# The attention product's way from PSUM into two time mixes, with a new order list and other cuts of the token axis

## The chip, the cores and the metric

The kernel runs on one core of a Trainium2 chip. The metric is the device time of one execution in microseconds (us). Engines go by the names of the profile: TensorE (PE, with its weight loads as PEld), VectorE (DVE), ScalarE (ACT), GpSimd (POOL) and SyncE (SP), which only issues transfers.

## The reference

Three stages follow each other. B = 2 batches, H = 12 heads, S = 448 tokens, D = 64.

```python
# 1: causal attention, float32
scores = q @ k.T / 8, masked above the diagonal; attn = exp(scores - rowmax)
attn = attn / (sum(attn) + 1e-9); x = (attn @ v) as (B, S, 768)

# 2: a feed-forward stage with a time mix
x_prev = x shifted by one token, a zero row first
xk = mu_k * x + (1 - mu_k) * x_prev
xr = mu_r * x + (1 - mu_r) * x_prev
v = relu(xk @ w_k) ** 2 @ w_v          # w_k 768 x 1024, w_v 1024 x 768
x = sigmoid(xr @ w_r) * v              # w_r 768 x 768

# 3: a feed-forward stage with a convolution over tokens
h = relu(x @ w_in); gate = sigmoid(conv3(h)); out = (h * gate) @ w_out
```

The weight matrices and the convolution weights arrive as 64-bit floats; the kernel turns them into 32-bit by integer steps.

## The kernel before

**Attention.** The 24 heads are worked as 12 jobs of two heads each: jobs 0 to 5 are batch 0, jobs 6 to 11 batch 1, and job i holds the 128 columns number i mod 6 of x. A job loads raw q and k (`Lk`) and v (`Lv`), transposes q and k on TensorE (`kqT`, line 313), copies them out of PSUM (`kC`), makes the scores in two groups (`sc.1`, `sc.2`, line 334), and for each of seven row blocks takes the row maximum with the mask (`red`, VectorE, line 347), the exponential with its sum (`exp`, ScalarE, line 356) and the scaling by the reciprocal sum (`norm`, line 72, 74 or 76 by engine). The scaled blocks are transposed (`T.a`, `T.b`, line 376), copied out (`C`), and multiplied with v into one PSUM bank po (`V.a`, `V.b`, line 404): x transposed, channels on the partitions, one zero column ahead of the 448 tokens, so that the shifted x is a slice of the same bank.

**The time mix.** From po, `mP.1` scales the shifted x by 1 - mu_r into a work tile m, `mD.1` adds mu_r times x (VectorE, line 429): that is xr. `mP.0` and `mD.0` do the same with mu_k into the kept tile `mixed`: that is xk. All four read po, so its bank is free when the fourth is done. `mH` and `mL` split xr into a high part (rounded to the format of the products) and a low rest; `k0` to `k11` with `H` and `L` do that for xk, once the attention's memory has been given over to the later stage (`act2`).

**Products.** Each product of the later stages is three matmuls (high by high, high by low, low by high; `mm3`, line 66). `pr e.b.c` is the part of xr @ w_r for output slice e, batch b and channel slice c; `E0` to `E3` are xk @ w_k for output slices 0 and 1 and both batches (PSUM tiles pk). In these the 896 tokens are cut as 448 and 448 (`TOK`). All later products cut them as 512 and 384 (`HALF`). A weight slice goes through the steps `L` (load), `a` (absolute value, ScalarE, line 137), `b`, `c`, `d`, `e` (integer steps), `h` and `l` (split).

**Order.** Around the change the order is written out by hand: in the string `ORDER` each word is one step, its engine after a slash (a, v or p), and TensorE, ScalarE, VectorE and GpSimd each run their steps in that order. SyncE's transfers are kept in the order of the text. After `E3` a planner orders the next stage (products pk and pv), and a second hand list orders the last one.

## Time and profile before

| | us |
|---|---|
| median of 3 runs | 354.12 (353.56 to 354.26) |
| the profiled execution, its own time | 353.53 |
| its span, first to last instruction | 351.8 |
| PE busy in the span | 345.7 |
| DVE busy | 307.2 |
| ACT busy | 235.2 |
| POOL busy | 94.9 |

The profile is of one execution. Busy times are sums over the span. Matmuls overlap each other, and their ends are modelled, so what a matmul costs is the distance from its start to the next start, and a busy PE can still hold short waits. On ScalarE and VectorE the end of one instruction overlaps the start of the next as well, and again the distance between starts is its cost.

### The profile page before, as it was taken

To read this page: it belongs to the slowest core of one execution; us is meant where nothing else is said; L and a number is where in the kernel's file an instruction comes from. 1 tells how busy PE (TensorE), PEld (TensorE's weight loads), DVE (VectorE), ACT (ScalarE), POOL (GpSimd) and SP (SyncE) were. 2 spreads that over 40 slices of the span, in tenths; PEclk is the share of its full clock that TensorE was granted. 3 is DMA by queue.
4 is the path that set the end of the run, shared out by engine and by line. 5 is a ranking of instruction groups with operands and counts; after the bars stand their busy time and mean duration, and the time that the engine had idled before them with its cause. 6 is when DMAs were issued, how large, how long until landed. Compare 5 with 4: busy or idle time off the path is not lost.

```text
span 351.8 us, 7217 instructions
## 1 busy us (share of the span) xinstructions
PE 345.7 (98%) x2682; PEld 309.5 (88%) x2682; DVE 307.2 (87%) x630; ACT 235.2 (67%) x515; POOL 94.9 (27%) x155
## 2 busy tenths in 40 slices
PE   8999999999999999999999999999999999999995
PEld 7678788888999998998888999998988999999995
DVE  3999999999989877989999997998998999898731
ACT  3999999999543276767886464345757878766501
POOL 8486986677535000000000000000000000368100
PEclk9999999999999999999999999999999999999999
DMA  7975855342033155446455434444231200379623
GB/s 180 250 161 124 203 137 163 76 133 76 11 93 113 56 179 181 131 140 238 155 174 182 148 100 170 150 133 167 89 108 73 89 2 0 67 135 214 128 89 135
DMA packets 60320, 45.33 MB, mean 129 GB/s; under 512 B 31608, under 2 KB 59036, under 8 KB 60284
## 3 DMA queue, kind: packets, MB, share of 16 engines
q1 hardware_dynamic: 56140, 39.90, 37.5%
q0 software_dynamic: 3216, 4.74, 7.3%
q8 instruction: 21, 0.34, 0.4%
q10 hardware_dynamic: 928, 0.23, 0.3%
q14 instruction: 15, 0.12, 0.1%
HBM read 38.17 MB, written 2.75 MB: 116 GB/s over the span
## 4 chain that ended last, share of the span: by engine, by line
PE 94%; ACT 2%; DVE 2%; POOL 1%; issue 0%; POOLq 0%
PE pk L66 17%; PE pv L66 16%; PE pr L66 13%; PE A L66 7%; PE po L404 6%; PE s L334 4%; PE B L66 4%; PE c L66 2%; PE D L66 2%; PE Yb L376 2%; PE Xa L376 2%; PE W L574 1%; PE q L313 1%; PE ph5l L66 1%; PE ph4l L66 1%; PE ph6l L66 1%
## 5 line engine op out<-in xcount | busy, mean ns | idle before, releaser
L903 POOL DMA_DIRECT2D s<-g x12 | 12.9, 1196 | 194.9 <-ACT st L87 188.6
L356 ACT ACTIVATE p<-e,st 128x448 f32<-128x448 f32 (+6 forms) x84 | 42.4, 514 | 1.9 <-DVE st L347 1.6
L72 POOL TENSOR_SCALAR p<-p,st 128x64 f32<-128x64 f32 (+6 forms) x70 | 34.7, 513 | 15.5 <-DVE st L347 6.1
L347 DVE CUSTOM_DVE_ANT_0 e<-s,mask 128x192 f32<-128x192 f32 (+6 forms) x84 | 31.5, 412 | 0.4 <-ACT p L356 0.4
L404 PE MATMUL po<-pt,v 128*64 128x128 f32 (+4 forms) x384 | 24.0, 277 | 0.0
L404 PEld LDWEIGHTS po<-pt,v 128*64 128x64 f32 x384 | 20.0, 137 | 3.3 <-issue 0.3
L334 PE MATMUL s<-kT,qT 64*64 64x384 f32 (+6 forms) x336 | 22.1, 386 | 0.7 <-DVE kT L79 0.5
L823 DVE SCALAR_TENSOR_TENSOR cv<-hT,cw,cv 128x448 f32<-128x448 f32 x32 | 21.5, 679 | 1.4 <-ACT cv L820 1.4
L334 PEld LDWEIGHTS s<-kT,qT 64*64 64x64 f32 x336 | 14.9, 132 | 6.8 <-ACT qT L79 0.9
L356 ACT ACTIVATION_READ_ACCUMULATOR p<-e,st 128x1 f32 x84 | 17.0, 202 | 0.0
L87 ACT ACTIVATE x<-xv 128x512 fp32r<-128x512 f32 (+1 forms) x12 | 6.8, 573 | 9.2 <-DVE xv L722 9.2
L91 POOL TENSOR_TENSOR xr<-m,xr 128x448 fp32r<-128x448 f32 x10 | 12.0, 1200 | 2.1 <-ACT xr L87 1.7
L1015 ACT ACTIVATE o<-A 128x384 f32<-128x384 f32 x3 | 1.5, 491 | 14.7 <-PE A L66 14.6
L827 ACT ACTIVATE cv<-cv 128x448 f32<-128x448 f32 x16 | 9.1, 571 | 3.2 <-DVE cv L823 3.2
L820 ACT ACTIVATE cv<-hT,cw 128x448 f32<-128x448 f32 x16 | 10.7, 668 | 0.5 <-DVE g L91 0.3
L829 DVE TENSOR_TENSOR cv<-cv,hT 128x448 f32<-128x448 f32 x16 | 9.9, 618 | 1.2 <-ACT cv L827 1.2
L903 POOL DMA_DIRECT2D wo6raw<-g x8 | 9.1, 1187 | 3.9 <-ACT wo6raw L928 3.9
L91 DVE TENSOR_TENSOR k<-a,k 128x512 fp32r<-128x512 f32 (+2 forms) x16 | 9.9, 617 | 0.0
L66 PE MATMUL pv<-k,wv0hl 128*128 128x512 f32 (+1 forms) x48 | 9.9, 364 | 0.0
L66 PE MATMUL pv<-k,wv4hl 128*128 128x512 f32 (+1 forms) x48 | 9.8, 363 | 0.0
L66 PE MATMUL pv<-k,wv2hl 128*128 128x512 f32 (+1 forms) x48 | 9.8, 363 | 0.0
L66 PE MATMUL pv<-k,wv3hl 128*128 128x512 f32 (+1 forms) x48 | 9.8, 363 | 0.0
(518 smaller groups left out, 1111.7 us busy)
## 6 DMA issues: line engine op xcount, KB each, us to landing
rqk<-in_q_dram SPq DMA_DIRECT2D x23, 112.0 KB, 3.4
v<-in_v_dram SPq DMA_DIRECT2D x24, 96.0 KB, 2.9
s<-g POOLq DMA_DIRECT2D x12, 192.0 KB, 3.8
rqk<-in_k_dram SPq DMA_DIRECT2D x16, 112.0 KB, 3.1
wo6raw<-g POOLq DMA_DIRECT2D x8, 192.0 KB, 4.9
wv0raw<-in_moe_w_v_dram SPq DMA_DIRECT2D x1, 1024.0 KB, 5.0
wv1raw<-in_moe_w_v_dram SPq DMA_DIRECT2D x1, 1024.0 KB, 4.6
wv2raw<-in_moe_w_v_dram SPq DMA_DIRECT2D x1, 1024.0 KB, 4.8
```

Of the source, the lines that this page charges most:

```text
L66: nc.tensor.matmul(ps_out, x, y, start=first and i == 0, stop=last and i == 2, skip_group_check=more,)
L72: nc.gpsimd.tensor_scalar(out_, in_, s, 1.0, ALU.mult, ALU.mult)
L91: e.tensor_tensor(out_, x, f32(h), ALU.subtract)
L334: nc.tensor.matmul(held[self.name(f"s{f}")][1][h, o:z], qT[r, i * LO:(i + 1) * LO], kT[r, :(i + 1) * LO], start=True, stop=True,)
L347: nc.vector.tensor_tensor_reduce(t[:, :w], used(self.name(f"s{f}"))[:, o:z], mask[:, S - w:], -SCALE, 3e38, ALU.add, ALU.min, self.st[:, 0 ...
L356: nc.scalar.activation(p[:, :w], self.s[i][:, :w], AF.Exp, bias=self.st[:, 0, i:i + 1], scale=-1.0, accum_out=self.st[:, 1, i:i + 1],)
L376: nc.tensor.transpose(o[:, u * LO:(u + 1) * LO], self.p[i][r, k0:k0 + P], ident[r, r])
L404: nc.tensor.matmul(self.T["po"][j * D:(j + 1) * D, 1 + i * LO - z:1 + (i + n) * LO], self.v[:, kc, j], self.T["pt"][:, a - z:a + n * LO], ...
L820: nc.scalar.activation(a, x[:, 0:S], AF.Copy, scale=cw[:, f:f + 1])
L823: nc.vector.scalar_tensor_tensor(a, x[:, j:S + j], cw[:, j * NF + f:j * NF + f + 1], a, ALU.mult, ALU.add)
L829: (nc.gpsimd if eng == "p" else nc.vector).tensor_tensor(a, a, hc, ALU.mult)
L903: nc.gpsimd.dma_start(out=dst, in_=f32(x), accum_op=ALU.add)
```

## The change

The product po is read three times instead of four: `xC` copies x (448 columns) from PSUM into `mixed`; `mP` makes the scaled shifted x for xr, from po (ScalarE, VectorE) or, where its engine is GpSimd, from the copy; `mD` adds as before. The key path's mix is now two steps of the k family on the copy: `P` scales the shifted copy into a work tile (447 columns) and scales column 0 in place, `D` adds mu_k times the copy in place (VectorE, both inputs in SBUF). These stand late in the order.

The cuts `TOK` give way to `PART`, 384 and 512 tokens, in the products pr, in E0 to E3, in the copies `sr` and in what reads pk 0 and 1; the second part holds the last 64 tokens of batch 0. In the new list five of the twelve `mP` run on GpSimd, four of nine weight slices do step `a` and four do step `h` on VectorE; ScalarE does 14 norms instead of 7; six of the twelve xk steps `H` are on VectorE and all twelve `L`; six of the xr steps `L` are on VectorE instead of two. The loads of job 1 stand ahead of those of job 0, and job 1 to 3's k loads are words of their own (`Lp`). The tiles of the later stage are all named at `act2`, in the order in which they were first used before; v's buffers are named ahead of those of raw q and k. The whole order list is new.

```diff
-    def narrow(step, dst, raw, eng="v"):
+    def narrow(step, dst, raw, eng=""):
 
         lo, hi = raw[:, 0::2], raw[:, 1::2]
         d = dst.bitcast(I32)
         if step == "a":
-            in_order(nc.scalar.activation(dst, hi.bitcast(F32), AF.Abs))
+            if eng == "v":
+                nc.vector.tensor_scalar(d, hi, as_int(0x7FFFFFFF), None, ALU.bitwise_and)
+            else:
+                in_order(nc.scalar.activation(dst, hi.bitcast(F32), AF.Abs))
+    vs = Kept(rawp, "v", 4, [P, NB + 1, 2, D], lambda t: [t[:LO, NB]])
...
     TOK = [slice(b * S, (b + 1) * S) for b in range(B)]
+    PART = [slice(0, 3 * P), slice(3 * P, NT)]
+
+    def width(t):
+        return t.stop - t.start
 ...
-    vs = Kept(rawp, "v", 4, [P, NB + 1, 2, D], lambda t: [t[:LO, NB]])
...
         def Lk(self):
             self.raw = first_qk if self.i == 0 else qks.get(self.i, self.name("rqk"))
-            other = nc.scalar if self.i == 0 else nc.gpsimd if self.i < 4 else nc.sync
-            for src, dst, e in ((q, self.raw[:LO], nc.sync), (k, self.raw[LO:], other)):
-                for j in range(2):
-                    if self.i or j == 0 or src is k:
-                        in_order(e.dma_start(out=dst[:, :, j], in_=half(src, self.b, 2 * self.hp + j)))
+            for j in range(2):
+                if self.i or j == 0:
+                    in_order(nc.sync.dma_start(out=self.raw[:LO, :, j], in_=half(q, self.b, 2 * self.hp + j)))
+            if self.i not in (1, 2, 3):
+                self.k_half(nc.sync if self.i else nc.scalar)
+
+        def Lp(self):
+            self.k_half(nc.gpsimd)
+
+        def k_half(self, e):
+            for j in range(2):
+                in_order(e.dma_start(out=self.raw[LO:, :, j], in_=half(k, self.b, 2 * self.hp + j)))
 ...
-                self.T["po"] = bank(self.name("po"), 4)
+                self.T["po"] = bank(self.name("po"), 3)
...
-        def mP(self, eng, kind):
-            kind = int(kind)
-            m = self.m(kind)
-            a = 2 * NC + kind * NC + self.hp
-            scaled(eng, m, used(self.name("po"))[:, :S], mu[:, a:a + 1])
-
-        def m(self, kind):
-            if not kind:
-                return mixed[self.hp][:, self.b]
-            if "m" not in self.T:
-                self.T["m"] = mslots.get(self.i, self.name("m"))
-            return self.T["m"][:, :S]
-
-        def mD(self, _, kind):
-            kind = int(kind)
-            m, a = self.m(kind), kind * NC + self.hp
-            nc.vector.scalar_tensor_tensor(m, used(self.name("po"))[:, 1:S + 1], mu[:, a:a + 1], m, ALU.mult, ALU.add)
+        def xC(self, eng):
+            copy(eng, mixed[self.hp][:, self.b], used(self.name("po"))[:, 1:S + 1])
+
+        def mP(self, eng):
+            self.T["m"] = t = mslots.get(self.i, self.name("m"))
+            x = 3 * NC + self.hp
+            po = used(self.name("po"))
+            if eng == "p":
+                nc.gpsimd.memset(t[:, :1], 0.0)
+                scaled(eng, t[:, 1:S], mixed[self.hp][:, self.b, :S - 1], mu[:, x:x + 1])
+            else:
+                scaled(eng, t[:, :S], po[:, :S], mu[:, x:x + 1])
+
+        def mD(self, _):
+            m, x = self.T["m"][:, :S], NC + self.hp
+            nc.vector.scalar_tensor_tensor(m, used(self.name("po"))[:, 1:S + 1], mu[:, x:x + 1], m, ALU.mult, ALU.add)
 
         def mH(self, eng):
-            mix_h(xr[self.hp], self.m(1), self.b, eng)
+            mix_h(xr[self.hp], self.T["m"][:, :S], self.b, eng)
 
         def mL(self, eng):
-            mix_l(xr[self.hp], self.m(1), self.b, eng)
+            mix_l(xr[self.hp], self.T["m"][:, :S], self.b, eng)
             mslots.put(self.i)
 
     def mix_h(dst, m, b, eng):
-        split_h("p" if eng == "p" else "s", dst[:, 0, TOK[b]], m)
+        split_h(eng, dst[:, 0, TOK[b]], m)
 ...
-                narrow(s, self.c[:, :n], self.raw.bitcast(I32)[:, :2 * n], eng or "v")
+                narrow(s, self.c[:, :n], self.raw.bitcast(I32)[:, :2 * n], eng)
...
-                split_h("s", self.t[:, 0, :n], self.c[:, :n])
+                split_h(eng, self.t[:, 0, :n], self.c[:, :n])
...
     ORDER = """
-        0:Lk W0 sm:L W*2 0:kqT 0:kC.k/a sm:a 1:Lk 0:kC.q/v W*2 0:sc.2 W*1 1:kqT sm:n 0:red.0 0:red.5 0:red.2 0:red.3
-        0:exp.0 0:sc.1 1:kC.k/v 2:Lk pads 0:exp.5 1:kC.q/a 0:exp.2 1:sc.2 0:red.6 0:exp.3 0:red.1 0:red.4 0:exp.1 0:exp.4
...
-        10:V.a w4:b/p w4:c 11:V.b 11:C.aX/a 11:V.a act2 11:mP.1/a 9:mD.1 pr0.1.0 pr0.1.1 w4:d 10:mP.1/v 9:mH/p
-        pr4.0.4 pr5.1.5 pr4.0.5 sr2.1/a pr5.0.4 w7:d sr4.1/v E0 sr5.1/a k10:L/v sr3.1/v k11:L/p sr4.0/a w8:b/v w8:c
...
+        1:Lk 1:Lp 0:Lk sm:L 2:Lk W0 W*2 0:kqT 0:kC.q/a 0:kC.k/v W*1 sm:a sm:n W*2 0:sc.1 0:red.1 1:kqT 0:red.6
+        0:sc.2 0:exp.1 1:kC.q/a 1:kC.k/v 1:sc.2 0:red.4 0:exp.6 0:exp.4 0:red.2 2:Lp 0:red.3 0:red.5 1:red.3
...
+        10:norm.2/p 10:T.b 11:exp.6 11:exp.5 10:norm.0/p 11:exp.1 10:T.a 11:rec 11:norm.5/p w0:h pr1.1.1 pr1.1.2
+        k8:D 10:C.bY/a 11:norm.6/p 11:Lv 11:norm.4/a 10:C.bX/a 11:norm.0/p w5:L 10:C.aY/a w4:c pr2.1.0 9:xC/v
+        9:mP/v 11:norm.1/p 9:mD sr2.0/a pr2.1.1 10:C.aX/a k2:D pr2.1.2 k5:P/a 11:T.a 9:mH/a w0:l/v 11:norm.3/p
+        11:norm.2/a 11:T.b k9:P/a 11:C.bX/a 11:C.aX/a 11:C.bY/a w4:d 10:Lv 10:V.a 11:C.aY/a 10:V.b 9:mL/v k5:D
+        k9:D k1:P/a 10:xC/a 11:V.b 11:V.a act2 k2:H/v w4:e w5:a w5:b/p k1:D 11:xC/a 11:mP/a 10:mP/v 10:mD k6:P/a
+        pr0.1.0 pr0.1.1 11:mD pr1.1.3 k6:D 10:mH/a 11:mH/a pr0.1.2 pr0.1.3 10:mL/v 11:mL/v w5:c pr2.1.3 pr2.1.4
...
+        k7:H/p k7:L/v w8:c k6:L/v pr5.1.3 pr5.1.4 pr5.1.5 pr5.0.4 pr5.0.5 k11:H/v k8:L/v pr4.1.3 k4:H/p pr4.1.4
+        k10:L/v k4:L/v pr4.1.5 w8:d k3:L/v w8:e w6:h/v w8:h/v w6:l/v sr5.1/v sr4.1/v sr5.0/v k11:L/v E2 E0
+        w8:l/v E3 E1
     """
...
-        products(held[f"pr{e}_{b}"][1][:, :S], [slices[e].t], xr, TOK[b], NC, c)
+        t = PART[b]
+        products(held[f"pr{e}_{b}"][1][:, :width(t)], [slices[e].t], xr, t, NC, c)
...
-        copy(eng, sr[e][:, TOK[b]], used(f"pr{e}_{b}")[:, :S])
+        t = PART[b]
+        copy(eng, sr[e][:, t], used(f"pr{e}_{b}")[:, :width(t)])
 
     def xk_step(x, s, eng):
         b, c = divmod(x, NC)
-        if s == "H":
-            if c not in xk:
-                xk[c] = big(f"X{c}", f"xk{c}")
-            mix_h(xk[c], mixed[c][:, b], b, eng)
-        else:
-            mix_l(xk[c], mixed[c][:, b], b, eng)
-
+        m = mixed[c][:, b]
+        if s == "P":
+            t = mslots.get(("k", x), f"mk_{x}")
+            scaled(eng, t[:, 1:S], m[:, :S - 1], mu[:, 2 * NC + c:2 * NC + c + 1])
+            scaled(eng, m[:, :1], m[:, :1], mu[:, c:c + 1])
+            mk[x] = t
+        elif s == "D":
+            nc.vector.scalar_tensor_tensor(
+                m[:, 1:], m[:, 1:], mu[:, c:c + 1], mk[x][:, 1:S], ALU.mult, ALU.add
+            )
+            mslots.put(("k", x))
+        elif s == "H":
+            mix_h(xk[c], m, b, eng)
+        else:
+            mix_l(xk[c], m, b, eng)
+
+    mk = {}
...
         elif what == "act2":
             actx.close()
             late.append(ctx.enter_context(tc.tile_pool(name="act2", bufs=1, reuse_waits="tile")))
+            for c in (1, 4, 0, 2, 5, 3):
+                xk[c] = big(f"X{c}", f"xk{c}")
+            for e in (4, 5, 3):
+                sr[e] = home(f"U{e}").tile([P, NT], F32, tag=f"U{e}", name=f"sr{e}")
         elif what[0] == "E":
             f, b = divmod(int(what[1:]), B)
-            pk_banks[f, b] = bank(f"pk{f}_{b}", 1)[:, :S]
+            t = PART[b]
+            pk_banks[f, b] = bank(f"pk{f}_{b}", 1)[:, :width(t)]
             for c in range(NC):
-                products(pk_banks[f, b], [slices[NE + f].t], [xk[i] for i in range(NC)], TOK[b], NC, c)
+                products(pk_banks[f, b], [slices[NE + f].t], [xk[i] for i in range(NC)], t, NC, c)
         elif what[:2] == "pr":
             xr_products(*(int(y) for y in what[2:].split(".")))
         elif what[:2] == "sr":
...
-                if op in ("Lk", "Lv"):
+                if op in ("Lk", "Lp", "Lv"):
...
-        pks = [(TOK[b], pk_banks[f, b]) for b in range(B)] if f < 2 else token_mm(f"pk{f}", w, xk, False)
+        pks = [(PART[b], pk_banks[f, b]) for b in range(B)] if f < 2 else token_mm(f"pk{f}", w, xk, False)
```

## Rows read from the trace of the kernel before

**Rows 1.** the page: busy time by engine; TensorE in 40 slices

```profile
PE 345.7 (98%) x2682; PEld 309.5 (88%) x2682; DVE 307.2 (87%) x630; ACT 235.2 (67%) x515; POOL 94.9 (27%) x155
...
PE   8999999999999999999999999999999999999995
```

**Rows 2.** busy us by stretch (instructions); then clock, DMA share, GB/s

```profile
10.00:75.00 65.00, 64.27 (x1083) 52.29 (x1079) 64.46 (x232) 64.12 (x201) 47.21 (x78) 1.00 0.60 148
75.00:89.80 14.80, 14.80 (x206) 12.96 (x206) 13.18 (x35) 13.69 (x37) 11.03 (x19) 1.00 0.36 117
89.80:136.00 46.20, 46.20 (x227) 41.97 (x224) 41.15 (x57) 21.91 (x36) 11.30 (x11) 1.00 0.32 103
```

**Rows 3.** chain of waits: start us, length us, engine, tile, line, pieces

```profile
89.91 30.57 PE pr L66 x147
120.47 3.72 PE pk L66 x18
...
124.81 54.77 PE pk L66 x270
179.58 58.03 PE pv L66 x288
```

**Rows 4.** TensorE by time: start us, length us, line, names, shapes, count

```profile
29.63 0.99 PE L334 MATMUL s<-kT,qT 64*64 64x384 f32 x16
30.55 0.27 PE L313 MATMUL q<-ident,rqk 64*128 64x64 f32 x1
...
48.58 1.75 PE L334 MATMUL s<-kT,qT 64*64 64x448 f32 x28
50.26 0.27 PE L376 MATMUL Xa<-ident,p 64*128 64x64 f32 x1
```

**Rows 5.** ScalarE by time, 60 to 64 us

```profile
60.60 0.62 ACT L356 ACTIVATE p<-e,st 128x384 f32<-128x384 f32 x1
...
61.21 0.67 ACT L356 ACTIVATE p<-e,st 128x448 f32<-128x448 f32 x1
...
61.86 0.63 ACT L76 ACTIVATE m<-po,mu 128x448 f32<-128x448 f32 x1
62.38 0.92 ACT L137 ACTIVATE wr3c<-wr3raw 128x768 f32<-128x768 f32 x1
63.19 0.35 ACT L356 ACTIVATE p<-e,st 128x64 f32<-128x64 f32 x1
```

**Rows 6.** ScalarE by time, 83 to 89 us

```profile
83.70 0.62 ACT L76 ACTIVATE p<-p,st 128x384 f32<-128x384 f32 x1
84.22 0.57 ACT L79 COPY pt<-Ya 128x512 f32<-128x512 f32 x1
...
88.09 0.59 ACT L79 COPY pt<-Xa 128x512 f32<-128x512 f32 x1
```

**Rows 7.** VectorE by time, 91 to 115 us

```profile
91.95 1.28 DVE L429 SCALAR_TENSOR_TENSOR m<-po,mu,m 128x448 f32<-128x448 f32 x2
...
107.55 1.79 DVE L144 SCALAR_TENSOR_TENSOR wk0c<-wk0raw,wk0c 128x768 int32<-128x768 int32 x1
109.26 1.57 DVE L91 TENSOR_TENSOR xk<-mixed,xk 128x448 fp32r<-128x448 f32 x1
110.75 0.95 DVE L146 SCALAR_TENSOR_TENSOR wk0c<-wk0raw,wk0c 128x768 int32<-128x768 int32 x1
...
113.96 1.15 DVE L91 TENSOR_TENSOR xk<-mixed,xk 128x448 fp32r<-128x448 f32 x2
```

**Rows 8.** GpSimd by time, 107 to 111 us

```profile
107.07 3.27 POOL L91 TENSOR_TENSOR xk<-mixed,xk 128x448 fp32r<-128x448 f32 x2
```

**Rows 9.** all engines by time, the start

```profile
0.74 0.73 SPq L299 DMA_DIRECT2D rqk<-in_q_dram  x1
...
4.97 0.27 PE L313 MATMUL q<-ident,rqk 64*128 64x64 f32 x1
```

**Rows 10.** transfers of raw q and k to 16 us: issue to landing

```profile
DMA to landing us min/median/max: 2.5/3.3/4.0
```

More of the change, by code (lines that the diff above doesn't have):

```diff
@@ L185, with __init__, get @@
     smp = actx.enter_context(tc.tile_pool(name="smp", bufs=1))
+    pads = []
+    class Kept(Slots):
+        def __init__(self, pool, tag, n, shape, zero):
+            self.free = [pool.tile(shape, F32, tag=f"{tag}_{i}", name=f"{tag}_{i}", bufs=1) for i in range(n)]
+            self.held = {}
+            for z in (z for t in self.free for z in zero(t)):
+                if pinned[0]:
+                    pads.append(z)
+                else:
+                    nc.gpsimd.memset(z, 0.0)
+        def get(self, key, name):
+            self.held[key] = t = self.free.pop(0)
+            return t
+    vs = Kept(rawp, "v", 4, [P, NB + 1, 2, D], lambda t: [t[:LO, NB]])
     qks = Slots(rawp, "qk", 3, [P, S // LO, 2, D])
@@ L251 @@
     ss = Slots(sp, "s", 5, [P, S])
-    pads = []
-    class Kept(Slots):
-        def __init__(self, pool, tag, n, shape, zero):
-            self.free = [pool.tile(shape, F32, tag=f"{tag}_{i}", name=f"{tag}_{i}", bufs=1) for i in range(n)]
-            self.held = {}
-            for z in (z for t in self.free for z in zero(t)):
-                if pinned[0]:
-                    pads.append(z)
-                else:
-                    nc.gpsimd.memset(z, 0.0)
-        def get(self, key, name):
-            self.held[key] = t = self.free.pop(0)
-            return t
-    vs = Kept(rawp, "v", 4, [P, NB + 1, 2, D], lambda t: [t[:LO, NB]])
     pslots = {
@@ new lines @@
+        1:mL/p 6:red.0 6:exp.0 2:mH/p 3:mH/p w2:d 5:C.bX/a 8:kqT 8:kC.q/a 8:kC.k/v 6:rec 6:norm.0/p 7:red.2
+        11:Lk 7:exp.5 7:red.1 7:exp.1 6:norm.6/p 7:exp.2 6:norm.5/a 7:red.0 4:V.a 5:C.bY/v 4:V.b 7:exp.0 4:xC/v
+        w3:L 8:sc.1 8:sc.2 7:exp.6 w1:l/p 7:red.3 7:exp.3 8:red.6 4:mP/a 8:red.5 5:V.b 7:red.4 8:red.3
+        6:norm.1/p 6:norm.4/v 8:red.0 7:exp.4 6:T.a 6:C.aY/a 5:V.a 6:norm.3/p 8:exp.0 6:norm.2/p 4:mD 8:red.2
+        6:T.b 7:rec 7:norm.3/p 6:C.aX/a 8:exp.2 2:mL/p 8:red.4 6:C.bX/v 7:norm.4/a 8:red.1 9:sc.1 6:C.bY/v
@@ new lines @@
+        8:norm.6/p 7:T.a 8:T.a 7:C.aY/a w2:h/v w3:b/p w3:c w2:l/p 8:Lv 10:sc.2 7:C.aX/a 6:xC/v 10:red.2 9:exp.0
+        10:sc.1 10:red.6 9:exp.6 10:red.3 9:exp.5 9:rec 9:norm.1/p w3:d 10:red.1 8:C.aY/a 6:mP/p 7:V.a w0:L
+        10:exp.2 7:V.b w3:e 8:C.aX/a 7:xC/v 9:norm.3/a 8:V.b w0:a 9:norm.4/p 9:norm.6/p 10:exp.6 8:V.a w0:b/p
+        9:norm.2/a 10:red.4 10:exp.3 10:red.0 8:xC/a 11:sc.1 11:red.6 7:mP/a 11:sc.2 10:exp.1 10:exp.0
+        9:norm.5/p 6:mD w3:h 10:exp.4 10:red.5 11:red.2 w0:c 7:mD pr2.0.0 w3:l/p pr2.0.1 pr2.0.2 10:exp.5
@@ L567 @@
+        pr5.1.0 w6:a w6:b/p w6:c k4:D w6:d sr4.0/v w7:l/v pr5.1.1 pr5.1.2 pr4.1.2 w6:e w8:L w8:a/v k9:L/v w8:b/v
+        k7:H/p k7:L/v w8:c k6:L/v pr5.1.3 pr5.1.4 pr5.1.5 pr5.0.4 pr5.0.5 k11:H/v k8:L/v pr4.1.3 k4:H/p pr4.1.4
+        k10:L/v k4:L/v pr4.1.5 w8:d k3:L/v w8:e w6:h/v w8:h/v w6:l/v sr5.1/v sr4.1/v sr5.0/v k11:L/v E2 E0
+        w8:l/v E3 E1
     """
```

83 lines of the change are left out of this document (34 added, 49 removed).

## The prediction

> **What bounds the kernel now.** I read the page first. PE is busy for 98% of the span, and after the first of 40 slices no slice but the last falls under nine tenths [rows 1]. So a microsecond is won only where TensorE gets less to do, or waits less. The busy time by stretch comes next, because the average hides three regimes [rows 2]. From 10 to 75 us PE, DVE and ACT are all busy for 64 of 65 us: the attention is balanced between three engines, and whichever gets more work sets its pace. From 75 to 89.8 us ACT and DVE have 1.1 and 1.6 us idle. From 89.8 to 136 us (the rest of the pr products, and E0 to E3) PE is never idle, ACT has half its time free, and DVE is busy for 41.15 of 46.20 us. The chain of waits, read last, says the same in order of time: from 89.91 us it is one run of PE's products [rows 3]. Behind 136 us the change edits only where two slices are cut, so I carry every difference at 136 us to the end.
>
> **The cuts of the token axis.** From 89.91 to 120.47 us 147 pr matmuls of 448 columns follow each other: 30.57 us, 208.0 ns each; E0 is 18 more in 3.72 us, 206.7 ns [rows 3]. The pv products, half of them 512 and half 384 columns, also 448 on the mean, take 58.03 us for 288, 201.5 ns each [rows 3]. The pk run between agrees: of its 270, 54 have 448 columns (54 by 207 is 11.2 us), which leaves 43.6 us for 216, or 201.8 ns. So a matmul of 448 columns costs 5.2 to 6.5 ns more than half a pair of 512 and 384. The change recuts 216 pr and 72 pk matmuls: 288 by these is 1.5 to 1.9 us less for PE. 222 of them stand behind the attention: 1.2 to 1.4 us there, and I take 1.4, by the nearer stretch.
>
> The Trainium skill has another rule: in "TensorE: Matmul & The Clock Gate", section "Wait — 56ns, not 53.3ns?", start to start is the columns over the clock plus a fixed 2.5 ns. By it both cuts cost the same and this term is nothing. The trace disagrees, 206.7 to 208.0 ns against 201.5 at the same mean width and a granted clock of 1.00 [rows 2, 3]; but those runs differ in stage as well as in width, so that no gain from the cuts stays a rival below.
>
> **TensorE in the attention.** The matmuls are the same. A block of scores alone takes 0.92 us (29.63 to 30.55), two together 1.68 (48.58 to 50.26) instead of 1.84 [rows 4]. The old list puts 8 such pairs side by side, the new one 11: 0.5 us less. The pr products before the attention's end are 66 of 448 columns before, and 54 of 384 and 18 of 512 after; per column as above that is 13.7 against 13.5 us. PE alone would be done with the attention 0.7 us earlier.
>
> **ScalarE in the attention.** Here the list moves work both ways. Ahead of the last product of job 11 it has 7 `mP` fewer, at 0.52 us (61.86 to 62.38) 3.6 us, and 5 weight steps fewer, at up to 0.81 us (62.38 to 63.19) 4.0 us [rows 5]. It gains 5 `xC`, plain copies of 448 columns from PSUM, bounded above by the scaled one's 0.52 [rows 5], which I put at 0.44, 2.2; 7 norms of mixed width, 0.52 us for 384 columns [rows 6] and at 64 no more than the 0.35 of an exponential [rows 5], 2.3; 4 steps `P`, each 0.52 us and a one-column step between nothing and 0.35 that I put at 0.2, 2.9; and 3 `mH` and 3 copies more, under the same bound, put at 0.45, 2.7. Together some +2.5 us, of which 1.1 us (the last `P` and `xC`) are not needed by the product. DVE's account to the same point is even: 7 fewer `mD`, 8 fewer `mP` and 6 fewer copies and norms, against 6 `xC`, 4 `D`, 4 `mL` and 6 weight steps.
>
> Before, ACT finished the last copy for job 11 at 88.09 plus 0.59 us [rows 6], and PE went over to the products at 89.9 [rows 3], 1.2 us later. ACT had 2.0 us idle between 10 and 89.8 [rows 2]. With 1.4 us more needed work it is done between 88.1 (it fills all its idle time) and 90.1 (none), and PE 1.2 us later, 89.3 to 91.3. I take the middle, 90.3: 0.4 us later than before, although PE alone would be earlier. A shorter queue on PE turns into waiting for ACT.
>
> **The xk steps behind the attention.** This is what the change adds in time. From job 11's `mD` to the last xk low part that the first product (now E2) needs, DVE has in list order 1 `mD` and 7 `D` at 0.59 us (1.28 less one overlap, for two [rows 7]), 2 `mL` and 11 `L` at 0.54, 5 `H` at 0.3, 3 copies `sr` at 0.54, and 18 weight steps, 12.8 us together (the dear kind is 0.95 us long and overlaps the next by 0.08 [rows 7]): 27.7 us. `D` reads only SBUF where `mD` reads PSUM; this stretch of the trace has no such step at this width, so the bounds are the subtraction's 0.54 and the 0.87 of the wider step [rows 7], over 7 of them -0.4 to +1.9 us, and I keep the 0.59 of the nearest kind; a copy `H` within SBUF lies between nothing and the subtraction's 0.54, and 0.3 is the middle. PE has from the attention's end to E2 54 products of 384 and 90 of 512 columns, 30.0 us. `mD` can begin 1.3 us behind that end (`xC` and `mP` in a row on ACT). So DVE is ready at 29.0, PE at 30.0: 1.0 us of slack. Before, the last such step ended at 115.11 us, and E0 began at 120.47: 5.4 us of slack [rows 3, 7].
>
> How much DVE loses on the way decides. Before, it spent 23.2 us (91.95 to 115.11) on 17.7 us of such work, 5.5 us lost, most of it beside GpSimd: while GpSimd runs two subtractions (107.07, 3.27 us [rows 8]) a step that is 0.95 us long elsewhere took 1.79 and one of 0.61 took 1.57 [rows 7]. The new list leaves GpSimd 2.4 us of steps in this stretch (3 `H`, 1 `b`) instead of 7.4, and no subtraction. A third of the loss is 1.8 us; I allow 1.3, as the long kind is gone, and E2 waits 0.3 us.
>
> The Trainium skill's rule on this, in "SBUF — State Buffer", section "Who interferes with whom": a VectorE instruction with two SBUF inputs shares a port with GpSimd's reads and one of the two waits it out. That fits the two long rows [rows 7, 8], and by it the new `D`, with two SBUF inputs, joins the steps that can be held up, where the old `mD` with one could not.
>
> **The start.** Job 0's first q load was SyncE's first, at 0.74 us [rows 9], and is now its third; each takes 0.7 us to issue, and 2.5 to 4.0 us to land [rows 10]. Before, the first transpose started at 4.97 us [rows 9]. The load now lands at 4.7 to 6.1 us: 0 to 1.1 us later, about 0.3. It pushes ACT as well, and lies within the bounds above.
>
> **Sum.** In the profiled execution: attention's end +0.4, products behind it -1.4, wait at E2 +0.3: -0.7 us, 352.8 against 353.53 (its span 351.8 and 1.7 us around it). The median of the runs shown lies 0.6 higher, at 354.12; less 0.7 that is 353.4.
>
> **Rivals.**
> - *TensorE keeps its own pace.* ACT fills its idle time and the start costs nothing: -0.7 at the attention's end, -1.4 behind it, no wait: -2.1, 352.0 us. For it: DVE's account is even and GpSimd's lighter. Against: ACT's 2.0 us of idle is spread over 80 us.
> - *VectorE becomes the bound at the first pk product* (slower). If DVE loses more than 1.0 us on the way to E2, PE waits for the rest; at the old 5.5 us, 4.5 us. Then +0.4 - 1.4 + 4.5 = +3.5, 357.6 us; at half of that loss +0.7, 354.8 us. It turns the balance from 2.0 us lost. For it: the slack falls from 5.4 to 1.0 us, and seven `D` are new. Against: GpSimd's share falls by two thirds.
> - *The cuts give nothing*, the old width being dear only for its stage: +0.4 + 0.3 = +0.7, 354.8 us. For it: no row shows both cuts in one stage. Against: pk before and behind 136 us has the same operands.
> - *The start is late by its whole bound*, 1.1 us, and nothing absorbs it: -0.7 + 0.8, 354.2 us.
>
> **How the numbers follow.** Forecast 0.40 (own range 352.4 to 354.4), TensorE's own pace 0.18, VectorE the bound 0.28, cuts worth nothing 0.07, late start 0.07. 0.2% (0.7 us) is about what a measurement of this kernel tells from no change. Faster by more: half of the forecast and all of the first rival, 0.39. Slower by more: most of the second rival, half of the third, and a little of the forecast, 0.32. Within: 0.29. The range, 351.6 to 356.6, reaches over the first rival and into the second.
>
> **What would show it.** pr matmuls starting 174 and 229 ns apart in the two parts (wrong at 180 and 235); the attention's last po matmul near 90.3 us, with ACT's last copy 1.2 us ahead of it; E2's first matmul with under 1 us of wait on a VectorE xk step, DVE without steps of twice their length before it; the first transpose at 5.0 to 5.6 us. A gap over 1.7 us ahead of E2, or an attention that ends past 91.3, would make the forecast wrong on the slow side; an end before 89.3 on the fast side.

## The result: 0.6% slower, with times that spread

| kernel | median us | lowest to highest | runs |
|---|---|---|---|
| before | 353.86 | 353.28 to 354.28 | 15 |
| changed | 355.44 | 354.56 to 358.23 | 16 |

The ratio is 1.0056, with a 95% interval of 1.0036 to 1.0076. The forecast was 353.4. The spread is a result too: 1.0 us before, 3.7 us now. The profiled executions show the difference in small, 354.85 against 353.53 us. Four executions of 682 to 1186 us (one each of the kernel before, cuts_alone, loose_p_late and load_lead_alone) and one of tok_cuts at 360.04 us are counted as slow and left out of every figure here.

The chain of waits of the changed kernel (start us, length us, engine, tile, line, pieces) answers to [rows 3]:

```profile
88.47 3.67 PE po L418 x64
92.15 30.20 PE pr L66 x144
122.35 58.05 PE pk L66 x288
180.40 58.03 PE pv L66 x288
```

The attention ends at 92.15 instead of 89.91 us: 2.24 later. From there to pv it takes 88.25 instead of 89.67 us, so 1.42 come back, and pv starts 0.82 later. The other 0.5 us between the two profiles lie behind that, 0.14 of them ahead of ScalarE's last step and the rest after it. There is no gap ahead of pk: the wait for VectorE that I had priced at 0.3, and made the main rival, isn't there. The last xk low part that VectorE makes ends about when pk begins, and its products come later:

```profile
121.66 0.61 DVE L91 TENSOR_TENSOR xk<-mixed,xk 128x448 fp32r<-128x448 f32 x1
```

The busy time by stretch, the attention in two and then what stands behind it, answers to [rows 2] (us, then PE, PEld, DVE, ACT, POOL; clock, DMA share, GB/s):

```profile
10.00:75.00 65.00, 62.43 (x1083) 51.03 (x1085) 63.96 (x239) 64.09 (x211) 49.65 (x82) 1.00 0.63 159
75.00:92.00 17.00, 16.70 (x219) 14.48 (x215) 16.59 (x33) 16.87 (x44) 9.11 (x17) 1.00 0.22 62
92.00:136.00 44.00, 44.00 (x219) 38.91 (x216) 41.69 (x69) 21.83 (x42) 4.22 (x5) 1.00 0.32 98
```

TensorE waits 2.57 us between 10 and 75 us, where it waited 0.73. ScalarE is as busy as before there, and busy to the end where it had 1.1 us idle. The start, answering to [rows 9]:

```profile
0.74 2.07 SPq L304 DMA_DIRECT2D rqk<-in_q_dram  x3
...
5.92 0.24 PE L327 MATMUL q<-ident,rqk 64*128 64x64 f32 x1 [1.02 <-DMA rqk<-in_q_dram]
```

The first transpose is 0.95 us later and PE waits 1.02 us for job 0's load. So the rival "late start" is in the profile nearly at its whole bound. What made the other 1.3 us of the later end, and the spread, the profile of one execution doesn't say.

### The profile page after: what moved, and what is told of

It reads as the page before. It is cut to its first block, busy times and chain, and to the rows that moved or that the text cites. A ratio compares the mean times of both kernels' runs of the same rounds, so it can differ in the third digit from the quotient of the medians.

```text
span 353.1 us, 7247 instructions
## 1 busy us (share of the span) xinstructions
PE 344.0 (97%) x2682; PEld 307.0 (87%) x2682; DVE 310.1 (88%) x643; ACT 237.3 (67%) x535; POOL 88.4 (25%) x151
## 4 chain that ended last, share of the span: by engine, by line
PE 82%; DVE 9%; ACT 6%; DMA 1%; issue 1%; SPq 0%; DVEq 0%
PE pk L66 16%; PE pv L66 16%; PE pr L66 9%; PE A L66 7%; PE po L418 4%; DVE e L361 4%; PE B L66 4%; PE s L348 3%; PE c L66 2%; PE D L66 2%; ACT p L370 2%; PE ph5l L66 1%; PE ph4l L66 1%; PE ph6l L66 1%; PE ph7l L66 1%; PE ph3l L66 1%
## 5 line engine op out<-in xcount | busy, mean ns | idle before, releaser
L370 ACT ACTIVATE p<-e,st 128x320 f32<-128x320 f32 (+6 forms) x84 | 42.8, 523 | 2.4 <-DVE st L361 1.6
L72 POOL TENSOR_SCALAR p<-p,st 128x256 f32<-128x256 f32 (+5 forms) x66 | 33.3, 521 | 12.3 <-DVE st L378 7.6
L741 ACT ACTIVATE a<-pk 128x384 f32<-128x384 f32 (+1 forms) x16 | 8.6, 536 | 24.8 <-PE pk L66 23.2
L348 PE MATMUL s<-kT,qT 64*64 64x448 f32 (+6 forms) x336 | 22.7, 386 | 1.3 <-DVE st L361 0.6
L370 ACT ACTIVATION_READ_ACCUMULATOR p<-e,st 128x1 f32 x84 | 17.8, 211 | 0.0
L390 PE MATMUL Yb<-ident,p 64*128 64x64 f32 x96 | 8.7, 228 | 1.2 <-DVE st L361 0.8
L91 DVE TENSOR_TENSOR k<-a,k 128x384 fp32r<-128x384 f32 (+1 forms) x16 | 9.9, 617 | 0.0
```

The source lines that it names most:

```text
L72: nc.gpsimd.tensor_scalar(out_, in_, s, 1.0, ALU.mult, ALU.mult)
L91: e.tensor_tensor(out_, x, f32(h), ALU.subtract)
L348: nc.tensor.matmul(held[self.name(f"s{f}")][1][h, o:z], qT[r, i * LO:(i + 1) * LO], kT[r, :(i + 1) * LO], start=True, stop=True,)
L370: nc.scalar.activation(p[:, :w], self.s[i][:, :w], AF.Exp, bias=self.st[:, 0, i:i + 1], scale=-1.0, accum_out=self.st[:, 1, i:i + 1],)
```

## The experiments

All medians in us; ratios are to the kernel before, run on the same chip beside them.

### Single parts: the start, ScalarE's key steps, the cuts

**q_first.** In the order list:

```diff
-1:Lk 1:Lp 0:Lk sm:L 2:Lk W0
+0:Lk 1:Lk 1:Lp sm:L 2:Lk W0
```

> The changed kernel with one edit: job 0's load is again issued ahead of job 1's. Theory 'start': the q load of job 0 is third on SyncE's queue and so the first transpose starts at 5.92 instead of 4.97 us, and nothing behind it absorbs that; then the first transpose is back at 4.9 to 5.1 us, the attention's last po matmul moves from 92.15 to about 91.2 us, and the time falls by 0.9 us. Rival 'absorbed': the ScalarE queue has idle time enough (0.8 us at 48 us, 1.2 in all), so that the start comes back but the attention's end stays at 92.0 to 92.2 us and the time within 0.2 us. Second question: whether the wide spread of the changed kernel's times (354.6 to 358.2 us) is made by the start; if so the runs here lie within 1 us of each other, if not they spread over 3 us as before.

355.07 (354.22 to 357.17), ratio 1.0035 (1.0020 to 1.0050): 0.37 us less than the changed kernel. The transpose is back at 5.06 us, the profiled attention's end is not earlier (92.56), and the spread stays, at 3.0 us. Neither theory holds whole: something between start and end swallows time, and not the same in every run.

**p_pool**, and **q_first_p_pool** with both edits:

```diff
-k2:P/a ... k5:P/a ... k9:P/a ... k1:P/a
+k2:P/p ... k5:P/p ... k9:P/p ... k1:P/p
```

> The changed kernel with one edit: the four steps P that ScalarE does ahead of or beside the last attention products (k2, k5, k9, k1) go to GpSimd, which is busy for 4.3 of the 10 us from 80 to 90. Each is 0.72 us from start to start for the 447 columns and 0.2 to 0.3 for the single column. Theory 'ScalarE': its added work sets the attention's end, so with three P of about 1.0 us fewer ahead of the last copy (3.0 us) the copy moves up by as much as the next bound allows: attention's end at 89.5 to 91.0 us instead of 92.15, time 1 to 2.5 us less. Rival 'GpSimd': the P delay GpSimd's norms of jobs 10 and 11 that the same products wait for, so the end stays at 92 us or comes later. Rival 'TensorE or VectorE': the end stays within 0.3 us, although ScalarE shows 2 to 3 us of new idle time ahead of it.

> Both edits of the two runs before. Theories 'start' and 'ScalarE' together: the attention's end at 88.9 to 90.2 us, time 352 to 353.3 us, 2 to 3.4 less than the changed kernel and below the kernel before. If ScalarE has slack once the P are gone, the start is absorbed and the sum is less than the two parts; if neither theory holds, the time stays at that of the changed kernel.

357.26 and 356.46, ratios 1.0091 (1.0075 to 1.0108) and 1.0076 (1.0064 to 1.0088). The rival GpSimd was right. The busy time of the same ten us, first in the changed kernel, then in p_pool (the columns as above):

```profile
80.00:90.00 10.00, 9.70 (x140) 8.05 (x141) 9.69 (x17) 9.90 (x26) 4.31 (x10) 1.00 0.35 102
```

```profile
80.00:90.00 10.00, 9.06 (x91) 7.26 (x89) 9.93 (x19) 8.14 (x20) 9.81 (x14) 1.00 0.36 103
```

GpSimd goes from 4.31 to 9.81 us, ScalarE loses 1.8, and TensorE waits for GpSimd's norms. Idle time of an engine in the share table is not room when the products wait for its queue.

**cuts_alone**, the kernel before with this:

```diff
-products(held[f"pr{e}_{b}"][1][:, :S], [slices[e].t], xr, TOK[b], NC, c)
+t = PART[b]
+products(held[f"pr{e}_{b}"][1][:, :width(t)], [slices[e].t], xr, t, NC, c)
...
```

> The kernel before with the token axis of pr and of the first two pk slices cut into 384 and 512 instead of 448 and 448, and nothing else of the change. Theory of the prediction: a matmul of 448 costs 5.2 to 6.5 ns more than half a pair of 384 and 512, 288 of them, 222 behind the attention: pr pairs start 174 and 229 ns apart, the first pk product (now E0) starts with no wait, and the time falls by 1.4 to 1.9 us, to about 352.2. Rival 'stage, not width': pairs still take 2 x 207 ns, time within 0.3 us. Rival 'no room': the earlier end of pr turns into a wait for VectorE at the pk products, of which 5.4 us were slack, so none is expected.

354.27, ratio 1.0013 (1.0005 to 1.0022): not faster. The price of the widths was right. This is E0 and E1 there, 18 products each (TensorE by time):

```profile
121.88 3.28 PE L66 MATMUL pk<-xk,wk0hl 128*128 128x384 f32 x18
...
125.52 4.28 PE L66 MATMUL pk<-xk,wk0hl 128*128 128x512 f32 x18
```

What follows them starts at 125.00 and 129.64 us, so that is 173 and 229 ns from start to start. But pr behind the attention takes longer now:

```profile
90.27 31.77 PE pr L66 x147
```

31.77 us for the 147 that took 30.57 [rows 3]. The first part of each pair (384 columns, cheap) stands mostly ahead of the attention's end, the second (512, dear) mostly behind it. What TensorE saves ahead of the end it spends waiting (from 10 to 90 us it is busy for 78.18 us, 79.27 in the kernel before), and what is dearer behind counts in full.

### Stalls in the attention, late key steps, the old cuts, the copy alone

**loose**, q_first with two moves:

```diff
-3:mH/p w2:d 5:C.bX/a ... 7:red.0 4:V.a ... 5:mD 5:mH/a 9:exp.2 ... 8:norm.0/a 9:red.3
+3:mH/p 5:C.bX/a ... 7:red.0 w2:d 4:V.a ... 5:mD 9:exp.2 ... 8:norm.0/a 5:mH/a 9:red.3
```

> Job 0's load first (as in q_first), and two moves in the list: the weight step w2:d behind seven score reductions instead of ahead of them, so that it no longer meets GpSimd's two copies 2:mH and 3:mH (beside them it took 1.94 us instead of 0.95, and ScalarE then stood still for 0.78 to 0.95 us near 48 us); and ScalarE's 5:mH two norms later, so that it doesn't wait for VectorE's 5:mD (1.18 us near 59 us in q_first, where VectorE was held up beside GpSimd's 5:mP and a subtraction). Theory 'shared stalls': what keeps the attention's end late is ScalarE waiting for VectorE where GpSimd holds VectorE up; then both stalls go, ScalarE's idle time from 10 to 90 us falls from 2.3 to under 0.5 us, the attention's last po matmul comes at 90.3 to 91.2 us instead of 92.3, and the time falls by 1.0 to 2.0 us against q_first, to 353 to 354. Rival 'conserved': the stall appears a few us later at another place and the end stays at 92 us, time within 0.3 us of q_first.

356.02 (354.37 to 357.00), ratio 1.0054 (1.0035 to 1.0073). The stall near 48 us went, and 1.2 us of ScalarE's idle time appeared near 60. That is the rival "conserved", but the time is 0.95 over q_first's, where it gave 0.3; six runs that spread over 2.6 us don't settle the difference. The stall itself is well shown by the changed kernel's VectorE and GpSimd rows:

```profile
45.60 1.94 DVE L147 SCALAR_TENSOR_TENSOR wr2c<-wr2raw,wr2c 128x768 int32<-128x768 int32 x1
```

```profile
45.61 1.12 POOL L83 TENSOR_SCALAR xr<-m 128x448 fp32r<-128x448 f32 x2
```

A step of 0.95 us takes 1.94 beside 1.12 us of GpSimd's copies; in loose, away from them, it takes 0.97. The Trainium skill says the same ("SBUF — State Buffer", "Who interferes with whom": a VectorE instruction with two SBUF inputs contends with a GpSimd instruction that reads SBUF); the 1.0 us lost here agrees with it.

**loose_p_late** moves k2, k5, k9 and k1 behind the attention, and five steps H and three h there from VectorE to ScalarE:

```diff
-k2:P/a ... k2:D ... k5:P/a ... k9:P/a ... k5:D k9:D k1:P/a ... 11:V.b 11:V.a act2 k2:H/v ... k1:D
+11:V.b 11:V.a act2 ... k1:P/a k6:H/a k3:P/a k1:D k0:P/a k1:H/a ... k2:P/a ... k5:P/a k2:D k2:H/a ... k9:P/a k5:D ... k9:D
...
```

> As loose, and the four key steps k2, k5, k9 and k1 (P and D) are done behind the attention, where ScalarE idles from 107 to 122 us; for this five copies H of xk and three h of weights go from VectorE to ScalarE there (2.9 us of VectorE's work out, four D of 0.6 us and none else in, as only two of the four D stood ahead of the attention's end). Theory 'ScalarE': with 3 us less of work ahead of job 11's last copy the attention's end moves up by another 1 to 2 us, to 88.8 to 90 us, and the time to 351.5 to 353. Rival 'TensorE': the end moves by less than 0.5 us since PE has no more than 1 to 2 us of waits left. Rival 'VectorE at pk': the first pk product waits for its xk, by over 0.5 us.

359.76 (358.74 to 361.30), ratio 1.0157 (1.0142 to 1.0172). The rival "VectorE at pk" was right: TensorE waits 2.57 us for a low part of xk inside pk.

**tok_cuts**, the changed kernel with the old widths:

```diff
-PART = [slice(0, 3 * P), slice(3 * P, NT)]
+PART = TOK
```

> The changed kernel with the old cut: pr and the first two pk slices 448 and 448 columns wide. By the prediction's term the time rises by 1.4 us (222 matmuls behind the attention, 6.5 ns each). But the change of a width also moves columns past the attention's end: ahead of it stand 54 products of the first part and 18 of the second (+33 and -23 ns each: +1.4 us of TensorE's work ahead, where it waits 2.9 us anyway), behind it 54 first and 90 second (+33 and -23: -0.3 us), and in pk 36 and 36 (+0.35 us). Theory 'absorbed': the time is within 0.5 us of the changed kernel's. Theory of the prediction: +1.4 us.

355.97, ratio 1.0055 (1.0039 to 1.0070), the changed kernel's 1.0056 again; the medians differ by 0.5 us, well within either spread. The chain:

```profile
93.19 29.95 PE pr L66 x144
123.13 58.25 PE pk L66 x288
```

88.19 us from there to pv, against 88.25 with the cuts: behind the attention they are worth nothing.

**copy_once_old_list**, in the list of before:

```diff
-i:mP.1/x  i:mP.0/y  i:mD.1  i:mD.0  kj:H
+i:mP/x    i:xC/y    i:mD            kj:P/a (two products ahead) kj:D kj:H
```

> The copy alone, in the order list of before and with its cuts of 448: each job's second scaled product and second mix from PSUM become one plain copy and nothing (at the places of mP.0), PSUM is given back after three readers, and the key's P and D stand behind 11:mL, one product or two ahead of each H. Ahead of the attention's end VectorE loses 8 mD of 0.59 us (4.7 us), ScalarE about 0.1 us per copy; behind it ScalarE gets 12 P of about 0.95 us (11.4 us into 15 us of idle time) and VectorE 8 more steps D of 0.6 us (4.8 us into 5.4 us of slack). Theory 'the copy is sound, the list is not': attention's end at 89.0 to 89.9 us, first pk product with 0 to 0.7 us of wait, time 353.0 to 354.2. Rival 'the copy itself costs': the first pk product waits for xk by 1.5 us or more and the time is over 355 us.

358.73, ratio 1.0125 (1.0106 to 1.0143): the rival. TensorE's rows there:

```profile
104.20 1.08 PE L66 MATMUL pr<-xr,wr4hl 128*128 128x448 f32 x4 [1.05 <-DVE wr4hl L91]
124.21 5.45 PE L66 MATMUL pk<-xk,wk0hl 128*128 128x448 f32 x18 [2.51 <-ACT sr L79]
```

The attention's end comes 0.3 us earlier, but the key steps in bulk behind it make VectorE late, and pr and pk wait. The wait of 2.51 us at pk goes by way of a load, in the chain of waits there:

```profile
118.11 4.56 DMA wk2raw<-in_moe_w_k_dram
122.75 0.90 ACT wk2c L140
123.65 0.43 ACT sr L79
```

The load of weight slice wk2 waits for VectorE's last step on the raw slice of wk0 and is issued at 118.1 us, in the kernel before at 111.8. ScalarE stands still for 3.77 us until it lands, and the copies `sr` that pk waits for stand behind that step in its list. So this old list, with the key steps at these places, doesn't carry the copy. Whether it would with other places, or with that load earlier, no run shows.

### The start again, and what spreads the times

**start_of_before** (changed kernel) and **before_load_1_first** (kernel before):

```diff
-1:Lk 1:Lp 0:Lk sm:L 2:Lk W0
+0:Lk sm:L 1:Lk 1:Lp 2:Lk W0
```

```diff
-0:Lk W0 sm:L W*2 0:kqT 0:kC.k/a sm:a 1:Lk
+1:Lk 0:Lk W0 sm:L W*2 0:kqT 0:kC.k/a sm:a
```

> The changed kernel with the first loads in the order of before: job 0's q, the three small loads, then job 1's q on SyncE (in q_first the two q loads of job 1 still stood ahead of the small ones, and job 0's last k half landed at 5.1 us instead of 4.9). Theory 'start and clock': the two early loads hold job 0's back, TensorE then stands idle or starts late just where its clock is to rise, and in some runs it stays at the low level past 8 us (p_pool and loose_p_late: the first twelve score matmuls took 1.36 us instead of 0.72, first exponential at 10.5 to 11.0 us instead of 9.0); that makes the spread of 3.7 us. Then the first transpose is at 4.9 to 5.1 us, all runs lie within 1.5 us of each other and the median falls by 1.0 to 1.8 us, to 353.6 to 354.4. Rival 'list': the attention's list swallows what the start gives back, as in q_first: median 354.9 to 355.4, with the spread of 3 us left.

> The kernel before with one edit, job 1's load ahead of job 0's. Theory 'start and clock': first transpose at 5.8 to 6.0 us, the time rises by 0.7 to 1.2 us in the median, to 354.6 to 355.1, and the runs spread over 2 us or more where they lie within 1.0 now. Rival 'absorbed by the old list': the attention of before has idle time on ScalarE behind 75 us (1.1 us) and the time stays within 0.3 us, with a spread of 1 us.

354.00 (353.29 to 358.33), ratio 1.0024 (1.0001 to 1.0047); and 355.19 (354.37 to 355.98), ratio 1.0041 (1.0025 to 1.0057). So the order of the first loads alone is worth 1.44 us in the median of the one kernel and 1.31 in the other, of the 1.58 us of the result. The second is clear of noise; the first hardly, as the intervals of the two ratios overlap. And q_first, where job 0's load also goes first, gave 0.37: the rest came with the three small loads that start_of_before puts ahead of job 1's as well, and no run separates these. The spread of 1.5 us that the theory gave was missed: four of the twelve runs of start_of_before are above 354.9 and two above 356, and the profiled one is one of the two. Its VectorE, ScalarE and TensorE:

```profile
57.42 0.89 DVE L138 TENSOR_SCALAR wr3c<-wr3raw 128x768 int32<-128x768 int32 x1 [2.07 <-POOL xr L91]
```

```profile
60.62 0.58 ACT L87 ACTIVATE xr<-m 128x448 fp32r<-128x448 f32 x1 [2.42 <-DVE m L442]
```

```profile
58.90 2.61 PE L66 MATMUL pr<-xr,wr1hl 128*128 128x384 f32 x7 [1.96 <-DVE st L361]
```

VectorE stands still for 2.07 us ahead of the first step on weight slice wr3. The releaser named is a subtraction of GpSimd's, done at 54.8 us; GpSimd's next one ends at 57.3, but it can't be that, since in early_loads (below) the same step starts before it. The view of the tile names the load:

```profile
L162 SPq DMA_DIRECT2D wr3raw<-in_moe_w_r_dram x1: 564/564/564, 50.4 to 50.4; - x1
L138 DVE TENSOR_SCALAR wr3c<-wr3raw x1: 892/892/892, 57.4 to 57.4; 128x768 int32<-128x768 int32 x1
...
DMA to landing us min/median/max: 7.0/7.0/7.0
```

Issued at 50.4, landed 7.0 us later, at 57.4: the very moment of the step. VectorE waits for the load of wr1 too, 0.7 us, and in q_first's profile 0.32 us at wr3, whose load took 6.7 us there. In the changed kernel's own profile the two loads land just in time: wr3 has 6.7 us and takes 6.0, wr1 5.7 and 5.4. The kernel before has the same load with 12.6 us of lead, and its first reader on ScalarE:

```profile
L159 SPq DMA_DIRECT2D wr3raw<-in_moe_w_r_dram x1: 553/553/553, 49.8 to 49.8; - x1
L137 ACT ACTIVATE wr3c<-wr3raw x1: 920/920/920, 62.4 to 62.4; 128x768 f32<-128x768 f32 x1
```

**warm_longer** (`W*2 0:kqT` becomes `W*2 W*3 0:kqT`):

> The changed kernel with six more of the matmuls on the constant tile ahead of the first transpose (0.21 us each at the low clock, 0.11 at the high one), which fill the 1.02 us that TensorE waits for job 0's q load; the first transpose comes at 5.9 to 6.3 us. Theory 'the gap delays the clock': without the gap TensorE goes to the short matmul in every run, the spread falls from 3.7 to under 2 us and the median by 0.3 to 1.0 us. Rival 'the spread is made later': spread and median stay, or the median rises by the 0 to 0.3 us of the later transpose.

355.10 (354.62 to 356.18), ratio 1.0039 (1.0027 to 1.0052): 0.3 less than the changed kernel and 1.6 us of spread, in six runs. It speaks for the gap, not firmly.

**no_p_on_scalar**, start_of_before without the scaled shifted part for four channel slices (`D` adds the copy itself in its place):

```diff
-if s == "P":
+if s == "P" and x in (1, 2, 5, 9):
+    pass
+elif s == "P":
...
```

> start_of_before with the past half of the key mix left out for k1, k2, k5 and k9 (ScalarE's four P; VectorE's D reads the copy in its place, so its work is the same). Compared with start_of_before, ScalarE has three P of 0.95 us less ahead of job 11's last copy. Theory 'ScalarE': attention's end 1.5 to 2.8 us earlier, time 1.5 to 2.5 us less. Rival 'VectorE' (busy for 97 to 99% of the attention): the end moves by less than 0.5 us and ScalarE shows 2 us and more of new idle time, ended by VectorE.

353.64 (352.88 to 355.76), ratio 0.9995 (0.9981 to 1.0009): 0.36 under start_of_before, less than the two intervals tell apart. With 2.0 us of idle time on ScalarE behind 75 us TensorE then is never idle there:

```profile
75.00:91.50 16.50, 16.50 (x216) 14.35 (x210) 16.43 (x32) 14.45 (x35) 9.20 (x17) 1.00 0.21 64
```

The profiled attention ends at 91.49 us. So ScalarE is not the one engine that sets the end; take its work away and TensorE's own stands behind it.

### The lead of the weight loads

**start_and_lead** and **load_lead_alone** move the reader instead of the load (with and without the start of before), **start_lead_loose** and **start_lead_tok** add to the first the moves of loose and the old cuts:

```diff
-10:Lk w3:a/v 8:exp.4 ... w2:h/v w3:b/p ... 1:norm.3/p w1:a/v 2:exp.1 ... 1:norm.4/p w1:b/p
+10:Lk 8:exp.4 ... w2:h/v w3:a/v w3:b/p ... 1:norm.3/p 2:exp.1 ... 1:norm.4/p w1:a/v w1:b/p
```

> start_of_before, and the first step on the weight slices wr3 and wr1 (VectorE's a, the first reader of the loaded slice) moved later in the list, directly ahead of each slice's step b: the load of wr3 then has some 20 us of lead instead of 6.7 to 7.0, that of wr1 7.5 instead of 5.8. Theory 'lead': VectorE, first in first out, stood at w3:a for the load (0 to 2.1 us in the profiles), ScalarE waited for VectorE, and where PE idled 2 us its clock fell too; so the long runs go: all within 1.0 us of each other, median 353.0 to 353.7, below the kernel before by 0.2 to 0.9 us. Rival 'clock at the start': the spread of 3 us stays although no profile shows VectorE waiting for a weight slice. Rival 'list': spread falls but the median stays at 353.9 to 354.2.

> The changed kernel with only the two steps w3:a and w1:a later; its first loads stay as they are. Theory 'lead': against the changed kernel's 355.44 the median falls by 0.3 to 1.0 us and the runs above 356.2 (a third of them) go, unless TensorE's clock rises late at the start, which stays possible here: the spread is under 2 us. If the lead has no part in it, spread and median stay at 354.6 to 358 and 355.4.

> start_and_lead with the two moves of loose (w2:d behind the reductions, 5:mH two norms later), which took ScalarE's stall near 48 us away but were then hidden by the wait for wr3. Theory 'shared stalls': 0.3 to 0.9 us less than start_and_lead, about 352.7. Rival 'conserved': within 0.2 us of it.

> start_and_lead with pr and the first two pk slices cut 448 and 448. Where the attention now runs without long waits, TensorE sets more of its pace, so that the 1.4 us that the cuts take from TensorE ahead of its end count. Prediction's term (all of it counts): 1.4 us over start_and_lead. Theory 'absorbed ahead, nothing behind' (behind the attention the cuts move 64 columns a product past its end: 90 second parts against 54 first ones, +0.1 us in all): 0 to 0.5 us over it.

358.59, 359.43, 356.09 and 358.87, with ratios of 1.0131, 1.0154, 1.0071 and 1.0147. The edit was bad: GpSimd's b now stood right behind the late a, in its queue ahead of other steps (here start_and_lead):

```profile
64.93 0.83 POOL L143 TENSOR_SCALAR wr3c<-wr3c 128x768 f32<-128x768 f32 x1 [2.04 <-DVE wr3c L138]
```

Two things follow all the same. The runs of the three with the start of before lie within 1.1, 0.8 and 0.3 us of each other, in four or five runs each, though a wait of 2 us is built in. And the old cuts cost 0.28 us here, not 1.4. The moves of loose gain 2.5 us here; as they gain nothing on early_loads below, that is most likely the harm of the edit made less. Because the edit was bad, load_lead_alone doesn't show what the lead alone, with the start as changed, is worth; no other run tries it.

**early_loads** moves the loads instead, on top of start_of_before, and **early_loads_loose** adds the moves of loose:

```diff
-11:Lk 7:exp.5 ... 4:xC/v w3:L 8:sc.1 ... 0:norm.4/p 5:Lk 2:kC.k/v ... 1:exp.2 w1:L 1:red.1
+w3:L 11:Lk 7:exp.5 ... 4:xC/v 8:sc.1 ... 0:norm.4/p w1:L 5:Lk 2:kC.k/v ... 1:exp.2 1:red.1
```

> start_of_before with two loads earlier on SyncE and no compute step moved: wr3's ahead of job 11's q and k (issued near 46 us instead of 50.4, needed at 55.6), wr1's ahead of job 5's (12 to 13 us instead of 15.0, needed at 20.7). Theory 'lead': VectorE no longer waits for a slice (its step on wr3 starts at once, 10 us behind the issue); the runs above 354.9 (4 of 12 in start_of_before, up to 358.3) go, the spread is under 1.2 us and the median 353.2 to 353.8, 0.1 to 0.6 us under the kernel before. Rival 'another source': 3 us of spread stay with no wait of VectorE for a slice.

> early_loads with the two moves of loose: w2:d behind the reductions and 5:mH two norms later. In early_loads the stall of ScalarE near 48 us should still be there (0.4 to 1.0 us). Theory 'shared stalls': 0.3 to 0.9 us under early_loads, 352.5 to 353.2. Rival 'conserved': within 0.2 us of it, as the products wait for GpSimd's norms or VectorE a few us later.

353.77 (353.19 to 354.30), ratio 0.9994 (0.9985 to 1.0003); and 354.23, ratio 1.0004 (0.9995 to 1.0013). "Lead" holds: 1.1 us of spread in eleven runs, none above 354.3, where start_of_before, without the two moves, spreads over 5.0. The load of wr3 has 9.4 us and needs 5.1:

```profile
L162 SPq DMA_DIRECT2D wr3raw<-in_moe_w_r_dram x1: 1236/1236/1236, 46.3 to 46.3; - x1
L138 DVE TENSOR_SCALAR wr3c<-wr3raw x1: 725/725/725, 55.7 to 55.7; 128x768 int32<-128x768 int32 x1
...
DMA to landing us min/median/max: 5.1/5.1/5.1
```

Its chain and its first stretch:

```profile
91.55 30.22 PE pr L66 x144
121.77 58.05 PE pk L66 x288
179.82 58.03 PE pv L66 x288
```

```profile
10.00:75.00 65.00, 62.62 (x1096) 51.19 (x1088) 63.91 (x238) 64.13 (x210) 50.26 (x83) 1.00 0.64 159
```

With the start of before and two loads put right the change costs and gains nothing that can be measured. Taking ScalarE's stall away as well gains nothing either. No version here beats the kernel before.

## Why the prediction was wrong

The step that failed is the attention's end. The forecast put it 0.4 us later, at 90.3 and between 89.3 and 91.3; the changed kernel's profile has 92.15, 2.24 later. The forecast let 1.0 of the 1.4 us of ScalarE's added work, and the late start with it, vanish in ScalarE's 2.0 us of idle time. Neither did. ScalarE's last copy for job 11, before at 88.09 [rows 6], is now

```profile
89.99 0.61 ACT L79 COPY pt<-Ya 128x512 f32<-128x512 f32 x1
```

It ends 1.92 us later than before. From ScalarE's first copy of job 0 (at 5.71 us before, 6.66 now) to the end of this one it is busy for 81.31 us instead of 80.43, and idle for 2.63 instead of 2.54: the start adds its whole 0.95 and the work its whole 0.9 (forecast 1.4). TensorE's end is 1.55 us behind the copy, not 1.2. This says where the time shows in one execution. Two things behind the result, the median and the spread, were then found by runs:

*The start.* The prediction said "0 to 1.1 us later, about 0.3 ... lies within the bounds above". The profile has 0.95; in the medians the order of the first loads is worth 1.44 us (start_of_before against the changed kernel) and 1.31 (the same kind of edit in the kernel before). It is more than the later landing. I gave it no line of its own in the sum, because I took ScalarE's idle time for a buffer.

*The lead of the weight loads*, a term that is missing. I counted the first steps on the slices that go to VectorE as work, 0.47 to 0.95 us each, and did not ask when their loads land. The list shows both: wr3 goes from 12.6 to 6.7 us between issue and reader, wr1 from 11.3 to 5.7. A late load blocks VectorE, first in first out, and with it the reductions, ScalarE's exponentials and TensorE. Put right, it takes the mean of the runs from 354.6 (start_of_before) to 353.7 and the median from 354.0 to 353.8: it makes the tail.

With both put right the kernel runs at 353.77, beside my 353.4, and the rest of the sum can be judged by itself, from early_loads' profile:

- *ScalarE and the attention's end.* Forecast 0.4 later, 89.3 to 91.3. It is still 1.6 later (91.55), outside. That ScalarE paces it is not shown: without four P the time falls by 0.36 and the end is 91.49, and without the stall near 48 us the time doesn't fall. What the trace does show is where TensorE falls behind. From the first transpose to the end it waits 2.97 us, 1.33 before, and 1.3 of the added 1.64 lie between 10 and 23 us, at three waits for VectorE:

```profile
13.63 1.74 PE L348 MATMUL s<-kT,qT 64*64 64x384 f32 x28 [0.55 <-DVE st L361]
16.91 0.27 PE L390 MATMUL Ya<-ident,p 64*128 64x64 f32 x1 [0.31 <-DVE cw L502]
21.88 0.24 PE L390 MATMUL Yb<-ident,p 64*128 64x64 f32 x1 [0.60 <-DVE st L361]
```

In that stretch VectorE and ScalarE are busy for 12.73 and 13.00 of 13 us. The first `xC` comes at 27.2 us, so these waits belong to the new order of the first jobs, not to the way from PSUM into the mixes. The changed kernel has them too. No run moves them: what holds the end at 91.5 stays open.
- *Products behind the attention.* Forecast -1.4; 88.27 us to pv instead of 89.67, also -1.4, but not by the cuts: that the number fits is luck. The widths cost what I said. My slip was to multiply the mean saving by 222, though 90 of the 144 pr products behind the end are the wide half. Six products fewer behind it (144 for 150, at 208 ns) are 1.25 of it: the list has moved them ahead of the end, where their time is part of the later end. The cuts give nothing there (88.25 us with them, 88.19 without).
- *E2.* Forecast 0.3 of waiting; none. VectorE is never idle from 110 to 122 us and is done just in time. The balance was as thin as I wrote: with the key steps of loose_p_late added pk waits 2.57 us.
- *The sum.* Forecast -0.7; early_loads' profile stands at +0.24, with the end 1.2 us dearer than forecast and the wait 0.3 cheaper. The late start was in the list of rivals with a chance of 0.07; its bound, 1.1 us, was the right size, but its time, 354.2, kept the -0.7 for the rest and falls 1.2 short of 355.44.
